# Stage order in blocks, later first weight loads and later group transposes in a one-core attention and expert kernel

## The chip, the cores and the metric

The kernel runs on one core of one Trainium2 chip. Its time is the device time of one execution in microseconds (us); the figure for the kernel before is the median of three runs. The engines are TensorE (PE for its matmuls, PEld for its weight loads), VectorE (DVE), ScalarE (ACT), GpSimd (POOL) and SyncE (SP), which issues the DMAs here. Each engine works through its own queue in order.

## The reference, cut to what matters

```python
scores = scale * np.matmul(q, k.transpose(0, 1, 3, 2))      # 4 x 8 heads, 576 x 64
scores = np.where(block_i >= block_j, scores, -1e9)          # 64-row blocks
attn = softmax(scores); attn_out = np.matmul(attn, v)
x = attn_out.transpose(0, 2, 1, 3).reshape(2304, 512)

P = np.exp(logits - logits.max())                            # logits = x @ w_gate, 8 experts
for _ in range(8):
    P /= P.sum(1, keepdims=True) + 1e-09
    P /= P.sum(0, keepdims=True) + 1e-09
    P *= N / E
for e in range(E):                                           # w1 512 x 1024, w2 1024 x 512
    out += P[:, e:e + 1] * (np.maximum(x @ w1[e], 0.0) @ w2[e])

h = np.maximum(out @ w_in, 0.0)                              # w_in 512 x 2048
return (h * h) @ w_out
```

The second layer's weights arrive as 64-bit numbers; `conv64` turns them into 32-bit ones on the chip while the first layer runs.

## The kernel before, in words

After attention the 2304 tokens are worked on in three groups of 768 tokens (six tiles of 128). A **stage** takes one slice of 256 hidden units for one group. The first layer has 32 stages for each group (8 experts, four slices each), the second has eight, so that there are 120 stages, numbered S = 0 to 119: 0 to 95 are the first layer, 96 to 119 the second.

The first half of a stage are seven **products** (`product(S, j)`, lines 305 to 307, tile `m` in PSUM): a Winograd-like form with seven instead of eight block products, each six matmuls of 384 columns (high and low parts, two halves of k). DVE adds the results up (line 311), ACT and DVE make the high and low part of the hidden units out of the sums: in the first layer ACT line 280 and DVE line 281, in the second DVE line 285 (square of the positive part), ACT line 286 and DVE line 287. The low part's instruction is kept back in a list `wait` and put into DVE's queue by `flush_wait()` at the next product or tile. The second half are six **output tiles** (`output(S, t)`, lines 367 to 369, tile `y`): each six matmuls of 512 columns, followed by one DVE instruction that adds the tile to `acc` (lines 380 and 387). Every output tile of a stage needs the hidden units of all seven products of it.

PE gets the products of stage S woven with the output tiles of stage S - 1, in the order that the string `WEAVE` spells: m is a product, t a tile. Each of these pieces is a beat; at each beat one step of the side work is put into the queues: the next stage's weights (`stage_work`, `conv_a` at lines 165 and 166, `conv_b` at 173 and 174, sums at 149), the forming of the next group's operand (`form`, lines 233 to 240, every 12 beats in the first layer and every 5 in the second), `conv64`, and in stages 5 to 9 `gating` (the eight rounds of normalising P), whose remaining steps are put in at once ahead of tile 0 of stage 8. PSUM holds five product tiles and three output tiles; `y` is shared by the transposes of `x2` and by gating.

At the end of a group's first layer (`s == NMOE - 1`) each finished tile of `acc` is transposed by PE (`x2`, lines 350 to 352, four matmuls, an ACT copy and a DMA), one tile after it was computed.

The attention runs over 16 pairs of heads with six steps r each. The products of stages 0 to 4 are filled in between its steps from about pair 9 on (`fill`, up to `split`). SP's queue first gets the operands of pair 0, then `load("w1", 0)`, `load("w2", 0)` and `load("w1", 1)` (line 137), then q and k of pair 1 (line 522) and v (line 530). A task that makes the first stage's weights (`start`) is stepped from r = `TASK0` on, two steps at a time.

Of the kernel before, what the change touches and what calls it, by code (L numbers as in the profile page):

```python
# [28 lines left out]
NMOE = 32  # L29
# [39 lines left out]

FILL = 1.05  # L70

TASKS = 2

TASK0 = 9
READY = 3

FIRST = (
# [2 lines left out]
)  # L80

WEAVE = "mmtmtmtmtmtmt"

DLO = (0, 3, 6, 9, 12)

# [4 lines left out]
EARLY = 4  # L90
# [5 lines left out]
def fused_kernel(ctx: ExitStack, tc: tile.TileContext, q, k, v, wg, w1, w2, u1, u2, ident, out):  # L96
# [32 lines left out]
    def load(nm, S):  # L129
        if S >= len(stages):  # L130
            return
        s = stages[S][1]
        if s >= NMOE:
            drain(slow)
        t = raw[nm, S] = rawp.tile([128, 1024], F32, tag=nm, name="raw" + nm, bufs=2 if nm == "w1" else 1)
        src = (w1 if nm == "w1" else w2)[s] if s < NMOE else wf[nm][s - NMOE]
        nc.sync.dma_start(out=t, in_=src)
# [133 lines left out]
    late = deque()  # L271
# [17 lines left out]
    def flush_wait():  # L289
        while wait:  # L290
            wait.popleft()()
# [52 lines left out]
    def x2(q, t):  # L344

        a = acc[q % 2][:, t]
        p = extra["py"].tile([128, 512], F32, tag="y", name="x2t")
        for kk in range(KD):
            d = slice(kk * 128, (kk + 1) * 128)
            nc.tensor.transpose(p[:, d], a[:, d], idn)  # L350
        nc.scalar.activation(out=a, in_=p, func=ACTF.Copy)
        nc.sync.dma_start(out=xdram[q + NG][:, t], in_=a)

    def output(S, t):
        g, s, q = stages[S]
        flush_wait()
        while S not in ready_b:
            assert step_of(side)
        first = q == 0 and s < 8
        if q == 0 and s == 8:  # L360
            drain(gate)
        pool, tag = (extra["py"], "y") if "py" in extra else (extra["ps"], "g")
        p = pool.tile([128, 512], F32, tag=tag, name="y")
        bh, bl = wb[S]
        for f in range(2):
            hh, hl = (z[:, t * 128:(t + 1) * 128] for z in ht[S][f])
            nc.tensor.matmul(p, hh, bh[:, f], start=(f == 0), stop=False)  # L367
            nc.tensor.matmul(p, hh, bl[:, f], start=False, stop=False)  # L368
            nc.tensor.matmul(p, hl, bh[:, f], start=False, stop=(f == 1))  # L369

        a = acc[1 if first and s >= 4 else q % 2][:, t]
        e = s // 4
        tile_no = g * GT + t
        pe = prob[:, tile_no, e % NEXP:e % NEXP + 1]
        if s == NMOE or (first and s % 4 == 0):
            nc.scalar.activation(out=a, in_=p, func=ACTF.Copy)
        elif s == 0:
            nc.scalar.activation(out=a, in_=p, func=ACTF.Copy, scale=pe)
        elif s > NMOE or first:
            nc.vector.tensor_tensor(out=a, in0=p, in1=a, op=ALU.add)  # L380
        else:
            if q == 0 and s == 8:
                nc.scalar.activation(out=a, in_=a, func=ACTF.Copy, scale=prob[:, tile_no, 0:1])
                nc.vector.scalar_tensor_tensor(
                    out=a, in0=acc[1][:, t], scalar=prob[:, tile_no, 1:2], in1=a, op0=ALU.mult, op1=ALU.add
                )
            nc.vector.scalar_tensor_tensor(out=a, in0=p, scalar=pe, in1=a, op0=ALU.mult, op1=ALU.add)  # L387
        if late:
            x2(*late.popleft())
        if s == NMOE - 1:  # L390
            late.append((q, t))
        if s == NST - 1:
            r0 = tile_no * 128
            nc.sync.dma_start(out=out[r0:r0 + 128, :], in_=a)
# [4 lines left out]
    def piece(fn, us=0.0, need=None):  # L399
        pieces.append((need, us, fn))  # L400

    def products(S):
        res = []
        for j in range(7):
            def fn(j=j):
                product(S, j)
                if j == 0:
                    load("w1", S + 2)
                else:
                    conv_a(S + 1, PRODUCTS[j - 1][1])  # L410
                if j == 6:
                    conv_a(S + 1, PRODUCTS[6][1])
            res.append((0, 1.03, fn))
        return res

    def outputs(S):
        return [(0, 1.37, lambda t=t: output(S, t)) for t in range(GT)]
# [9 lines left out]
    def step_of(queue):  # L427
        while queue:
            if next(queue[0], "end") != "end":
                return True  # L430
            queue.popleft()
        return False

    def drain(queue):
        while step_of(queue):
            pass
# [17 lines left out]
    def begin(S):  # L454
        side.append(stage_work(S))
        g, s, q = stages[S]
        layer = s >= NMOE
        at, every = FORM[layer]
        if s - (NMOE if layer else 0) == at and q + 1 < 2 * NG:
            forming.append(fetch(q + 1))  # L460
            pace[0] = every

    for S in range(len(stages) + 1):
        a = products(S) if S < len(stages) else []
        b = outputs(S - 1) if S else []
        if a:
            piece(lambda S=S: begin(S))
        for z in WEAVE:
            src = a if z == "m" else b
            if src:  # L470
                pieces.append(src.pop(0))
        pieces += a + b
        if S == EARLY:
            split = len(pieces)
# [23 lines left out]
    def attention():  # L498
        with ExitStack() as es:
# [17 lines left out]
            def load_qk(n):  # L517
                for nm, src, w in (("k", k, SEQ), ("q", q, 9 * 128)):
                    t = qkv.tile([128, w], F32, tag=nm, name=nm)
                    raws[nm, n] = t  # L520
                    if n:
                        nc.sync.dma_start(out=t, in_=src[n])
                if n == 0:

                    for nm, c0, c1 in FIRST:
                        nc.sync.dma_start(out=raws[nm, 0][:, c0:c1], in_=(q if nm == "q" else k)[0, :, c0:c1])

            def load_v(n):
                t = raws["v", n] = vp.tile([128, 640], F32, tag="v", name="v")
                nc.sync.dma_start(out=t, in_=v[n])  # L530
# [134 lines left out]
            def logits_part(n):  # L665

                b, kk = divmod(n, 4)
                p = ps.tile([128, 512], F32, tag="g", name="lp")
                u = max(9 * b, 2 * GT)
                todo = []  # L670
                while u < 9 * (b + 1):
                    t, h = divmod(u, 2)
                    m = min(2 - h, 9 * (b + 1) - u)
                    todo.append((t, slice(64 * h, 64 * (h + m)), u - 9 * b, m))
                    u += m
                for t, rows, i, m in todo:
                    nc.tensor.matmul(
                        p[rows, t * NEXP:(t + 1) * NEXP], xs[:, i:i + m].rearrange("p b c -> p (b c)"),
                        wgt[:, kk], start=True, stop=True,
                    )  # L680
                while todo:
                    rows, t0 = todo[0][1], todo[0][0]
                    while todo and todo[0][1] == rows:
                        t1 = todo.pop(0)[0] + 1
                    o = prob[rows, t0:t1]
                    x = p[rows, t0 * NEXP:t1 * NEXP].rearrange("p (t e) -> p t e", e=NEXP)
                    if kk == 0:
                        nc.vector.tensor_copy(out=o, in_=x)
                    else:
                        nc.vector.tensor_tensor(out=o, in0=x, in1=o, op=ALU.add)  # L690
# [11 lines left out]
                nc.gpsimd.memset(pb[:, POFF[b] + width(b):POFF[b] + width(b) + 64], 0.0)  # L702
            nc.sync.dma_start(out=idn, in_=ident)
            nc.sync.dma_start(out=wgt, in_=wg)
            load("w1", 0)
            load("w2", 0)
            load("w1", 1)
            total = PAIRS * R
            budget = [0.0]
            later = []  # L710
# [15 lines left out]
            def do_fill(r):  # L726
                if r >= TASK0:
                    for _ in range(TASKS):
                        step_of(tasks)
                budget[0] = min(budget[0] + FILL, 2.0)  # L730
                if budget[0] > 0 and formed:
                    budget[0] = fill(budget[0], split)
# [23 lines left out]
            def do_loads(r):  # L756
                n, i = divmod(r, R)
                if later:
                    logits_part(later.pop())
                if i == 0 and n + 1 < PAIRS:  # L760
                    load_qk(n + 1)
                if r >= VSTEP and (r - VSTEP) % R == 0 and (r - VSTEP) // R < PAIRS:
                    load_v((r - VSTEP) // R)

# [141 lines left out]
```

## Time and profile before

| | before |
|---|---|
| median of three runs | 2143.82 us (2142.67 to 2145.21) |
| profiled execution: its time, its span | 2144.16 us, 2142.4 us |
| PE busy | 2105.8 us, 98% |
| PE weight loads busy | 1845.3 us, 86% |
| DVE busy | 1590.9 us, 74% |
| POOL busy | 1575.3 us, 74% |
| ACT busy | 916.2 us, 43% |
| mean granted TensorE clock | 0.995 of 2.4 GHz |

The span runs from the first to the last instruction of the profiled execution. PE's busy time is a sum of matmuls that overlap, with ends that are modelled: where PE sits at 100%, its pace is read from the distance between the starts of matmuls, not from how long each is shown. In a timeline a line shows the start, the length, the engine, the line of the program and, in brackets, how long the engine had been idle and what released it.

### The profile page before, as it was taken

The numbers are of one execution on the slowest core, as the hardware profiler recorded it, in microseconds if no ns is written. First come the engines' busy times: TensorE is split into PE (matmuls) and PEld (weight loads), VectorE is DVE, ScalarE is ACT, GpSimd is POOL, SyncE is SP. The second block draws the span as 40 slices with busy tenths as digits, with TensorE's granted clock in tenths as the row PEclk, the third lists the DMA queues.
The fourth block names the chain that finished last, engine by engine and source line by source line (L and its number), as shares of the span: only waits on it lengthen the run. The fifth ranks groups of instructions, "written<-read, shape, count | busy, mean of one in ns | idle before, by whom it ended". The sixth has DMA issues, their size and how long they took to land.

```text
span 2142.4 us, 32197 instructions
## 1 busy us (share of the span) xinstructions
PE 2105.8 (98%) x10835; PEld 1845.3 (86%) x10835; DVE 1590.9 (74%) x2890; ACT 916.2 (43%) x2267; POOL 1575.3 (74%) x1767
## 2 busy tenths in 40 slices
PE   8999999999999999999999999999999999999998
PEld 6777888888888988888889889898888888888887
DVE  6666678777778667778777767777887667878776
ACT  7766443334343443333434344343343443343432
POOL 3264465878888777778888767778787768878874
PEclk9999999999999999999999999999999999999999
DMA  4433122232232322332323233233222232131211
GB/s 159 136 103 116 53 69 69 89 108 90 84 99 74 120 92 84 99 104 84 99 84 99 79 109 99 84 108 95 87 85 70 70 104 74 64 123 60 99 60 50
DMA packets 80710, 194.58 MB, mean 91 GB/s; under 512 B 26144, under 2 KB 27296, under 8 KB 80544
## 3 DMA queue, kind: packets, MB, share of 16 engines
q1 hardware_dynamic: 80544, 192.53, 28.2%
q8 instruction: 85, 1.39, 0.3%
q14 instruction: 81, 0.66, 0.1%
HBM read 169.95 MB, written 20.97 MB: 89 GB/s over the span
## 4 chain that ended last, share of the span: by engine, by line
PE 88%; DVE 8%; ACT 2%; issue 1%; POOL 0%; DMA 0%; SPq 0%; DVEq 0%; POOLq 0%; ACTq 0%
PE y L369 14%; PE y L368 14%; PE y L367 14%; PE m L306 12%; PE m L307 12%; PE m L305 12%; PE sc L540 3%; PE pv L650 2%; PE T L610 2%; DVE c L285 2%; DVE h L287 2%; DVE c L311 1%; ACT h L286 1%; DVE acc L380 1%; DVE mu L311 0%
## 5 line engine op out<-in xcount | busy, mean ns | idle before, releaser
L367 PE MATMUL y<-b,h 128*128 128x512 f32 x1440 | 566.8, 394 | 19.2 <-ACT h L286 18.0
L369 PE MATMUL y<-b,h 128*128 128x512 f32 x1440 | 574.7, 399 | 0.3 <-DVE h L281 0.3
L305 PE MATMUL m<-x,ah 128*128 128x384 f32 x1680 | 569.9, 339 | 0.0
L368 PE MATMUL y<-b,h 128*128 128x512 f32 x1440 | 569.0, 395 | 0.0
L306 PE MATMUL m<-x,ah 128*128 128x384 f32 x1680 | 566.4, 337 | 0.0
L307 PE MATMUL m<-x,al 128*128 128x384 f32 x1680 | 562.8, 335 | 0.0
L166 POOL TENSOR_TENSOR al<-sum,ah 128x256 fp32r<-128x256 f32 x480 | 391.4, 830 | 223.7 <-ACT ah L165 203.2
L280 ACT ACTIVATE h<-c 128x384 fp32r<-128x384 f32 x384 | 201.8, 526 | 739.5 <-DVE c L311 739.4
L387 DVE SCALAR_TENSOR_TENSOR acc<-y,prob,acc 128x512 f32<-128x512 f32 x516 | 383.9, 744 | 80.0 <-PE y L369 79.0
L166 POOL TENSOR_TENSOR al<-raww,ah 128x256 fp32r<-128x256 f32 x360 | 296.6, 824 | 189.9 <-ACT ah L165 144.6
L281 DVE SCALAR_TENSOR_TENSOR h<-c,h 128x384 fp32r<-128x384 f32 x384 | 275.4, 717 | 187.1 <-ACT h L280 186.7
L306 PEld LDWEIGHTS m<-x,ah 128*128 128x128 f32 x1680 | 316.3, 188 | 34.9 <-issue 1.8
L305 PEld LDWEIGHTS m<-x,ah 128*128 128x128 f32 x1680 | 316.4, 188 | 31.4 <-issue 1.1
L174 POOL TENSOR_TENSOR b<-raww,b 128x512 fp32r<-128x512 f32 x240 | 324.4, 1352 | 20.7 <-ACT b L173 20.1
L369 PEld LDWEIGHTS y<-b,h 128*128 128x128 f32 x1440 | 270.1, 188 | 65.1 <-DVE h L287 5.9
L367 PEld LDWEIGHTS y<-b,h 128*128 128x128 f32 x1440 | 270.9, 188 | 61.1 <-ACT h L286 24.2
L307 PEld LDWEIGHTS m<-x,al 128*128 128x128 f32 x1680 | 316.0, 188 | 0.0
L368 PEld LDWEIGHTS y<-b,h 128*128 128x128 f32 x1440 | 270.3, 188 | 35.2 <-issue 0.9
L165 ACT ACTIVATE ah<-sum 128x256 fp32r<-128x256 f32 x480 | 183.5, 406 | 147.1 <-POOL sum L149 142.6
L149 POOL TENSOR_TENSOR sum<-raww 128x256 f32<-128x256 f32 x240 | 213.4, 889 | 0.0
L311 DVE TENSOR_TENSOR c<-m,u 128x384 f32<-128x384 f32 x240 | 131.9, 550 | 38.7 <-PE m L307 38.4
L173 ACT ACTIVATE b<-raww 128x512 fp32r<-128x512 f32 x240 | 148.7, 620 | 0.0
(90 smaller groups left out, 2264.5 us busy)
## 6 DMA issues: line engine op xcount, KB each, us to landing
raww<-w_t SPq DMA_DIRECT2D x192, 512.0 KB, 3.6
raww<-w1f SPq DMA_DIRECT2D x24, 512.0 KB, 3.3
raww<-w2f SPq DMA_DIRECT2D x24, 512.0 KB, 3.3
q<-q_d SPq DMA_DIRECT2D x15, 576.0 KB, 4.5
raw<-w_in_bits SPq DMA_DIRECT2D x16, 512.0 KB, 5.1
raw<-w_out_bits SPq DMA_DIRECT2D x16, 512.0 KB, 4.6
acc<-xd SPq DMA_DIRECT2D x30, 256.0 KB, 4.2
v<-v_p SPq DMA_DIRECT2D x16, 320.0 KB, 4.9
```

Of the source, the lines that this page charges most:

```text
L149: nc.gpsimd.tensor_tensor(out=t[:, o], in0=x, in1=y, op=op)
L166: nc.gpsimd.tensor_tensor(out=lo, in0=src, in1=hi.bitcast(F32), op=ALU.subtract)
L174: nc.gpsimd.tensor_tensor(out=lo[:, f], in0=src, in1=hi[:, f].bitcast(F32), op=ALU.subtract)
L280: nc.scalar.activation(out=hh, in_=x3, func=ACTF.Relu)
L281: wait.append(lambda: nc.vector.scalar_tensor_tensor(out=hl, in0=x3, scalar=0.0, in1=hh.bitcast(F32), op0=ALU.max, op1=ALU.subtract,))
L305: nc.tensor.matmul(p, ah[:, k2], bh[:, k2], start=(k2 == 0), stop=False)
L306: nc.tensor.matmul(p, ah[:, k2], bl[:, k2], start=False, stop=False)
L307: nc.tensor.matmul(p, al[:, k2], bh[:, k2], start=False, stop=(k2 == 1))
L367: nc.tensor.matmul(p, hh, bh[:, f], start=(f == 0), stop=False)
L368: nc.tensor.matmul(p, hh, bl[:, f], start=False, stop=False)
L369: nc.tensor.matmul(p, hl, bh[:, f], start=False, stop=(f == 1))
L387: nc.vector.scalar_tensor_tensor(out=a, in0=p, scalar=pe, in1=a, op0=ALU.mult, op1=ALU.add)
```

## The change

Three things are changed. From stage 5 on a stage's pieces are put into PE's queue as four products, three tiles, three products and three tiles (`BLOCKS`) instead of woven one by one; stages 0 to 4 keep `WEAVE`. The loads of the first two stages' weights are taken out of the head of SP's queue and put at step 3 of pairs 1, 2 and 3, and the task that uses them starts at r = 15 instead of 9. The transposes of a group's tiles come two tiles later than before while the group's last stage runs.

```diff
+WFIRST = {1: ("w1", 0), 2: ("w2", 0), 3: ("w1", 1)}
-TASK0 = 9
+TASK0 = 15
 WEAVE = "mmtmtmtmtmtmt"
+BLOCKS = "mmmmtttmmmttt"
...
-        if late:
-            x2(*late.popleft())
         if s == NMOE - 1:
             late.append((q, t))
+        if len(late) > (2 if s == NMOE - 1 else 0):
+            x2(*late.popleft())
...
-        for z in WEAVE:
+        for z in WEAVE if S <= EARLY else BLOCKS:
             src = a if z == "m" else b
             if src:
                 pieces.append(src.pop(0))
...
             nc.sync.dma_start(out=wgt, in_=wg)
-            load("w1", 0)
-            load("w2", 0)
-            load("w1", 1)
...
                 if i == 0 and n + 1 < PAIRS:
                     load_qk(n + 1)
+
+                if i == 3 and n in WFIRST:
+                    load(*WFIRST[n])
```

## Rows read from the trace of the kernel before

**Rows 1.** Page, part 1: engine, busy us, share of the span, instructions.

```profile
PE 2105.8 (98%) x10835; PEld 1845.3 (86%) x10835; DVE 1590.9 (74%) x2890; ACT 916.2 (43%) x2267; POOL 1575.3 (74%) x1767
```

**Rows 2.** Timeline of PE, one first-layer stage: start, length, instruction.

```profile
1000.81 0.33 PE L305 MATMUL m<-x,ah 128*128 128x384 f32 x1
...
1002.89 0.39 PE L367 MATMUL y<-b,h 128*128 128x512 f32 x1
...
1004.28 0.33 PE L305 MATMUL m<-x,ah 128*128 128x384 f32 x1
...
1016.45 0.33 PE L305 MATMUL m<-x,ah 128*128 128x384 f32 x1
```

**Rows 3.** Waits of PE, whole span: us in total, times, longest us.

```profile
PE y L367 <- ACT h L286: 18.0, 17, 2.0
```

**Rows 4.** Timeline of PE: second layer's first product; one stall of its stages.

```profile
1724.47 0.33 PE L305 MATMUL m<-x,ah 128*128 128x384 f32 x1
...
1811.47 0.50 PE L367 MATMUL y<-b,h 128*128 128x512 f32 x1 [1.98 <-ACT h L286]
```

**Rows 5.** Timeline of PE, the closing tiles: second tile, sixth, last matmul.

```profile
2131.64 0.39 PE L367 MATMUL y<-b,h 128*128 128x512 f32 x1
...
2137.09 0.39 PE L367 MATMUL y<-b,h 128*128 128x512 f32 x1
...
2138.22 0.39 PE L369 MATMUL y<-b,h 128*128 128x512 f32 x1
```

**Rows 6.** Timeline of PE, a group's end: one transpose and the next tile.

```profile
722.51 0.60 PE L350 MATMUL x2t<-idn,acc 128*128 128x128 f32 x4
...
724.00 0.39 PE L367 MATMUL y<-b,h 128*128 128x512 f32 x1
```

**Rows 7.** Groups of DVE, stage 109 (1945.1 to 1962.7): busy us, mean ns, idle before.

```profile
L285 DVE SCALAR_TENSOR_TENSOR c<-c 128x384 f32<-128x384 f32 x5 | 5.4, 1074 | 0.2
L380 DVE TENSOR_TENSOR acc<-y,acc 128x512 f32<-128x512 f32 x6 | 4.1, 679 | 0.0
L287 DVE TENSOR_TENSOR h<-c,h 128x384 fp32r<-128x384 f32 x4 | 3.2, 803 | 1.9 <-ACT h L286 1.8
L311 DVE TENSOR_TENSOR c<-m,u 128x384 f32<-128x384 f32 x2 | 1.1, 550 | 0.2 <-PE m L307 0.2
```

**Rows 8.** Waits of DVE, whole span.

```profile
DVE h L287 <- ACT h L286: 55.0, 93, 0.6
```

**Rows 9.** Timeline of DVE, last stage, line 285 while POOL is idle.

```profile
2122.77 0.56 DVE L285 SCALAR_TENSOR_TENSOR c<-c 128x384 f32<-128x384 f32 x1
```

**Rows 10.** Stage 109: us, busy of PE, PEld, DVE, ACT, POOL; clock, DMA share, GB/s.

```profile
1945.10:1962.70 17.60, 16.06 (x80) 13.95 (x79) 15.08 (x23) 6.91 (x17) 15.65 (x17) 1.00 0.18 61
```

**Rows 11.** Timeline, last stage: first matmuls of a tile and of the product behind.

```profile
2121.98 0.39 PE L367 MATMUL y<-b,h 128*128 128x512 f32 x1
...
2123.37 0.33 PE L305 MATMUL m<-x,ah 128*128 128x384 f32 x1
```

**Rows 12.** Stretch in the last stage, columns as in rows 10.

```profile
2120.00:2128.00 8.00, 8.00 (x41) 7.07 (x39) 5.64 (x11) 1.05 (x2) 0.00 (x0) 1.00 0.01 2
```

**Rows 13.** Timeline of PE: first scores of attention pairs 1, 2 and 3.

```profile
14.82 1.43 PE L540 MATMUL sc<-k,q 128*128 128x128 f32 x4 [2.39 <-DMA q<-q_d]
...
27.59 1.03 PE L540 MATMUL sc<-k,q 128*128 128x128 f32 x4
...
38.88 1.03 PE L540 MATMUL sc<-k,q 128*128 128x128 f32 x4
```

**Rows 14.** Timeline of SP's queue: the three first weight loads.

```profile
5.44 1.38 SPq L137 DMA_DIRECT2D raww<-w_t  x3
```

**Rows 15.** Stretches behind two stalls, columns as in rows 10.

```profile
15.40:18.80 3.40, 3.40 (x12) 2.66 (x11) 1.51 (x7) 1.57 (x5) 0.00 (x0) 0.51 0.63 242
...
356.70:360.20 3.50, 3.50 (x12) 3.11 (x11) 2.23 (x4) 2.66 (x6) 2.74 (x4) 0.51 0.01 2
```

**Rows 16.** Timeline, gating's last product of sums ahead of tile 0 of stage 8.

```profile
355.61 0.39 PE L827 MATMUL gc<-cs,ones 128*128 128x8 f32 x2 [3.15 <-DVE cs L823]
```

## The prediction

> **What bounds the kernel now.** I read the page first: PE is busy for 98% of the span [rows 1], so only two things can pay: gaps in PE, and PE's own pace. The pace is read from a timeline of PE in a quiet first-layer stage [rows 2]: the first product of one stage starts at 1000.81, that of the next at 16.45, so a stage lasts 15.64 us. Two products in a row take 2.08 (1000.81 to 1002.89), a tile 1.39 (1002.89 to 1004.28); 7 x 1.04 + 6 x 1.39 = 15.62 is the stage. Nothing is waited for, and the first layer repeats this length nearly everywhere; there an order of pieces can gain only if it changes the pace itself.
>
> Then the waits of PE: 18.0 us in 17 waits of the first matmul of a tile for the high part of the second layer's hidden units [rows 3], up to 2 us each [rows 4]. How much of the second layer that is: from its first product at 1724.47 [rows 4] to the last matmul at 2138.22 [rows 5] are 413.75 us. 24 stages of 15.64 are 375.4, the six closing tiles without their last matmul 6 x 1.39 - 0.23 = 8.1, six group transposes 6 x 0.45 = 2.7 (one transpose and a product take 1.49 [rows 6], less 1.04). What is left, 27.6 us, are these stalls with the slow matmuls behind them. So the second layer is paced by the chain product, DVE sum, square, ACT copy, low part, tile, and the first layer by PE alone.
>
> **Order in blocks: the second layer's stalls.** Before, between the end of a stage's last product and its first tile lie one old tile and two products, 1.39 + 2.08 = 3.5 us. In blocks there lie three tiles and four products, 3 x 1.39 + 4 x 1.04 = 8.3 us. I walk DVE's queue from the start of the block of three products, with the durations of a crowded stage [rows 7]: sums 0.55, square 1.07, low part 0.80, tile 0.68. Product 1 is there at 1.2 (1.04 and the hand-over, an estimate); sum, square, two sums, low part, square, sum, low part, square end at 8.2; ACT's copy keeps DVE waiting 0.59 [rows 8], the last low part ends at 9.6, the first tile's add at 10.3. The next stage's tiles start at 3.1 + 4.2 + 4.2 = 11.4. The hidden units (9.6) and the first of the three y buffers (10.3) are in time, by 1.1 us. In the same order only one of the four 0.59 waits is left in a stage; the others now have sums of the next product behind them.
>
> Two things stay late. At the very end six tiles follow directly on three: the closing tile 0 starts at 7.2 on that scale and needs tile 3's buffer, free at 8 with 0.56 for squares and low parts [rows 9] and POOL idle, at 10 otherwise: 1 to 2 us, 1.5 taken. And where the next group's operand is formed (14 parts, one every 5 beats of 13, so 5.4 stages in each of two groups), DVE has 7 x 0.55 + 4 x 1.07 + 4 x 0.80 + 6 x 0.68 + 0.55 + 0.59 = 16.5 us of work in a stage of 15.5: its lag grows 1.0 a stage, 5.4 in a group, of which 1.1 is slack: 9 us lost in the two groups at this end. With 0.56 for all eight it has 13.6 and loses nothing. The measured stage held 15.08 of DVE work [rows 10]; with one wait that is 15.7, near the pace, so I take 2.5. Gain: 27.6 - 1.5 - 2.5 = 23.6, between 16.6 and 26.6.
>
> **Order in blocks: PE's pace.** A tile between two products takes 1.39, also in the last stage [rows 11], where POOL does nothing and ACT 1.05 of 8 us [rows 12]. Six closing tiles follow one another, and there the second to sixth start 2131.64 to 2137.09 apart, 5.45 / 4 = 1.36 each [rows 5]. DVE's adds are present in both, so it is the change between products and tiles that costs, not a neighbour engine. In blocks four of six tiles follow a tile: 4 x 0.0275 = 0.11 a stage. For products the rows' rounding leaves 0 to 0.04; I take 0.015. 115 stages (5 to 119) x 0.125 = 14.4, less the 11 forming stages that DVE may pace (1.4): 13.0, between 0 and 14.4.
>
> The Trainium skill (TensorE: Matmul & The Clock Gate, section "Wait — 56ns, not 53.3ns?") says that back-to-back matmuls start N / 2.4 GHz + about 2.5 ns apart, N alone deciding. By that rule no order changes the pace, this term is 0 and the sum 13 smaller. The trace does not follow it here: 1.39 and 1.36 for the same six matmuls of 512 columns [rows 5, 11].
>
> **First loads.** Pair 1's first scores waited 2.39 us for q [rows 13]. Ahead of it in SP's queue stood three weight loads, 1.38 us of issue [rows 14] and 1.5 MB of transfer. Without them q is issued 1.4 earlier and shares the DMA engines with 1.5 MB less; the stall goes. Behind this idle time TensorE's clock was granted at 0.51, its lower level of 1.2 GHz, for 3.4 us [rows 15], and pair 1 took 12.77 against 11.29 of pair 2 [rows 13]: 1.5 more. Gain 2.39 to 3.9 if the clock holds, less up to 0.2 for the task's ACT and POOL steps, which move from pairs 1 and 2 to pairs 2 and 3, where they find the same gaps beside the softmax. I take 3.3 (2.2 to 3.9). The moved loads have free buffers, so nothing in SP's queue (q, k and v of a pair ahead, the attention's stores) stands behind a wait; w1 is read six steps, some 11 us, after its issue. Products only start after pair 8, so the later task delays none. If the loads did crowd pair 2's q, a stall like the 2.39 would be back.
>
> **Gating.** Tile 0 of stage 8 now comes after four products of stage 9 instead of two, so two more of gating's 60 steps are already in the queues when the rest is put in. PE waited 3.15 there for the reciprocal, product and sums on DVE [rows 16]; now only the fourth product's sum and the column sums are left, some 2 us. The clock fell to 0.51 behind it too [rows 15]; 3.5 us at half pace cost 1.7. Against it: the other rounds' sums meet runs of products, where DVE is busiest; up to 1. Gain 1.5 (-1 to 3).
>
> **Transposes two tiles later.** Four small matmuls a tile as before; no queue gets more. The transpose now needs a y buffer while tiles come in threes: after tile 4 it takes tile 3's, which DVE frees up to 0.4 late. The copy and store come two tiles later, but the group is read back only a layer of stages later. Cost 0.5 for three groups, 0 to 2.
>
> **Sum.** 23.6 + 13.0 + 3.3 + 1.5 - 0.5 = 40.9. From the profiled execution's 2144.16 that is 2103.3; the median lies 0.3 below it: **2103**.
>
> **The rivals.**
> The pace doesn't follow the order: 1.36 belongs to the quiet end. For it: in the closing tiles POOL and ACT are silent throughout. Against: they nearly were in a stretch with the slow tiles [rows 11, 12]. The 13.0 fall away: 2116.
>
> DVE becomes the bound of the forming stages. For it: squares take 1.07 with POOL on and 0.56 with POOL off [rows 7, 9], POOL holds 15.65 of 17.60 us [rows 10], and a faster PE squeezes both into less. If the low parts stretch like the squares, DVE needs 7 x 0.55 + 8 x 1.07 + 4.1 + 0.55 + 0.59 = 17.6, the old length: 5.4 x 2.1 less the slack of 1.1 are 10.2 us a group, 20.4 in two, of which 2.5 + 1.4 are counted above: 2120. The Trainium skill (SBUF — State Buffer, section "Who interferes with whom") names the reason: a VectorE instruction with two SBUF inputs and a GpSimd one that reads SBUF take the shared port exclusively, one fully waiting. The stretch from 0.56 to 1.07 agrees. Both rivals together: 2132.
>
> Slower: tiles in threes outrun DVE. Place: the first tile of each block of three, which needs the buffer of the first tile of the block before. In the first layer DVE frees it about 5 us early by the walk above, so it decides only once DVE's lag in every stage passes 5 us, as with the 64-bit conversion and the group operand on top. With stages of 15.5 + 0.5 = 16.0 the 91 first-layer stages cost 91 x 0.36 = 33 us more; the second layer, before at 15.64 + 27.6 / 24 = 16.8, would give back 19 and the start 3: 2155.
>
> Nothing: the stalls return at the blocks' ends and the pace stays: 2142.
>
> **How the numbers follow.** Forecast 0.65 (its own range 2095 to 2111), pace 0.13 (2116), DVE 0.12 (2120), both 0.02 (2132), slower 0.05, nothing 0.03. Faster by over 0.2% (4.3 us, about what a measurement of this kernel can tell from no change): 0.92, same 0.03, slower 0.05. The range takes in the forecast with its bounds and the first two rivals: 2094 to 2121.
>
> **What would show it.** Stage length: 15.52 in the first layer (15.64 if the pace rival holds); tiles 1.39, 1.36, 1.36 in a block. Waits of PE for line 286: under 3 us in all, or late in the forming stages. Second layer to the last matmul: 388 to 390 us. No wait of PE for q at pair 1, pair 1 near 11.3, no low clock there; gating's wait near 2. Wrong, if PE waits for DVE at a block's first tile, or if first-layer stages are longer than 15.64.

## The result, and the profile after

The changed kernel takes 2110.98 us (median of four runs, 2110.31 to 2112.36) against 2143.24 us before: 0.985 of the time, 95% interval 0.984 to 0.986, so 32 us less. The forecast was 2103, with a range of 2094 to 2121; without the rivals' times its range was 2095 to 2111, and the result lies at the upper end of that. The profiled execution has a span of 2109.7 us, 32.7 less than before, and all that follows divides these 32.7 up.

The page's first part, as in [rows 1]: PE is at 99%, and DVE is busy for 59 us longer with the same 2890 instructions.

```profile
PE 2086.4 (99%) x10835; PEld 1846.3 (88%) x10835; DVE 1650.1 (78%) x2890; ACT 921.2 (44%) x2267; POOL 1565.5 (74%) x1767
```

Two groups of DVE account for these 59 us (39 and 27 more; all others together lose 7): the low parts of the first layer and the squares of the second. The lines show the count, the busy time and the mean in ns of one, first of the kernel before, then of the changed one.

```profile
L281 DVE SCALAR_TENSOR_TENSOR h<-c,h 128x384 fp32r<-128x384 f32 x384 | 275.4, 717 | 187.1 <-ACT h L280 186.7
L285 DVE SCALAR_TENSOR_TENSOR c<-c 128x384 f32<-128x384 f32 x96 | 72.6, 756 | 3.3
```

```profile
L284 DVE SCALAR_TENSOR_TENSOR h<-c,h 128x384 fp32r<-128x384 f32 x384 | 314.8, 831 | 6.9 <-ACT h L283 5.1
L288 DVE SCALAR_TENSOR_TENSOR c<-c 128x384 f32<-128x384 f32 x96 | 99.5, 1036 | 1.7
```

Both kinds read two operands from SBUF. The adds of a tile, which read one of theirs from PSUM, kept their means of 744 and 682 ns. The squares will matter below.

First I looked for the waits of PE over the whole span (us in total, times, longest). The 18.0 us behind ACT's line 286 of [rows 3] are gone, the wait for q of [rows 13] too. In their place stands DVE's line 383, the add that frees a tile's buffer: 3.7 of its 5.6 us fall in the second layer, 1.9 in stages 5 to 8, where gating runs.

```profile
PE y L370 <- DVE acc L383: 5.6, 8, 1.6
...
PE x2t L353 <- ACT acc L354: 2.2, 1, 2.2
PE gc L830 <- DVE cs L826: 2.1, 1, 2.1
PE y L370 <- DVE acc L390: 1.0, 2, 0.5
```

Then PE's pace, in the timeline of a quiet first-layer stage, as in [rows 2]. The rows are the first matmul of product 1, of product 2, of tiles 1, 2 and 3, of the product behind them, and of the next stage:

```profile
993.48 0.33 PE L308 MATMUL m<-x,ah 128*128 128x384 f32 x1
994.55 0.33 PE L308 MATMUL m<-x,ah 128*128 128x384 f32 x1
...
997.67 0.39 PE L370 MATMUL y<-b,h 128*128 128x512 f32 x1
...
999.06 0.39 PE L370 MATMUL y<-b,h 128*128 128x512 f32 x1
...
1000.43 0.39 PE L370 MATMUL y<-b,h 128*128 128x512 f32 x1
...
1001.79 0.33 PE L308 MATMUL m<-x,ah 128*128 128x384 f32 x1
...
1009.05 0.33 PE L308 MATMUL m<-x,ah 128*128 128x384 f32 x1
```

A stage lasts 993.48 to 1009.05, 15.57 us; it was 15.64. Its three tiles take 1.39, 1.37 and 1.36, within a hundredth of the forecast. But the first product takes 1.07, and so does each first product behind tiles (1.066, by the distances between starts in the trace; before it was 1.044). The other engines are busier than in the stretch of [rows 12] (the stage's length, then busy time of PE, PEld, DVE, ACT and POOL, the granted clock, DMA share and GB/s):

```profile
993.48:1009.05 15.57, 15.57 (x79) 14.09 (x78) 13.62 (x21) 6.32 (x15) 14.21 (x16) 1.00 0.20 64
```

The second layer, from its first product to the last matmul, as in [rows 4, 5], now takes 392.1 us instead of 413.75; 388 to 390 were forecast. Its two largest waits for a tile's buffer stand between the ends, in the first stages of the second and third group (104 and 112), each at the first tile of a block:

```profile
1713.39 0.33 PE L308 MATMUL m<-x,ah 128*128 128x384 f32 x1
...
1848.68 0.47 PE L370 MATMUL y<-b,h 128*128 128x512 f32 x1 [1.22 <-DVE acc L383]
...
1976.03 0.47 PE L370 MATMUL y<-b,h 128*128 128x512 f32 x1 [1.61 <-DVE acc L383]
...
2105.52 0.39 PE L372 MATMUL y<-b,h 128*128 128x512 f32 x1
```

The start: the first scores of pairs 1, 2 and 3, as in [rows 13], and a stretch of pair 1 (busy time of PE, PEld, DVE, ACT, POOL, then the granted clock, DMA share and GB/s). Pair 1 starts at 12.26 instead of 14.82, takes 11.07 instead of 12.77, and the clock stays at its full level.

```profile
12.26 1.03 PE L543 MATMUL sc<-k,q 128*128 128x128 f32 x4
...
23.33 1.03 PE L543 MATMUL sc<-k,q 128*128 128x128 f32 x4
...
34.35 1.03 PE L543 MATMUL sc<-k,q 128*128 128x128 f32 x4
```

```profile
12.20:15.60 3.40, 3.40 (x23) 2.48 (x20) 3.37 (x17) 3.28 (x10) 2.10 (x3) 1.00 0.75 246
```

By the starts of the stages' first products the 32.7 us divide up so (gains are positive):

| term | forecast | measured |
|---|---|---|
| second layer's stalls | 23.6 | 22.3 |
| PE's pace in 115 stages, 0.067 each | 13.0 | 7.7 |
| start, up to stage 5 | 3.3 | 5.2 |
| gating, stages 5 to 10, both included | 1.5 | -0.5 |
| transposes, three groups | -0.5 | -4.0 |
| single stalls of six other first-layer stages | not counted | 2.0 |
| sum | 40.9 | 32.7 |

### The profile page after: what moved, and what is told of

The parts are those of the page before. It is cut to its first block, busy times and chain, and to the rows that moved or that the text cites. A ratio compares the mean times of both kernels' runs of the same rounds, so it can differ in the third digit from the quotient of the medians.

```text
span 2109.7 us, 32655 instructions
## 1 busy us (share of the span) xinstructions
PE 2086.4 (99%) x10835; PEld 1846.3 (88%) x10835; DVE 1650.1 (78%) x2890; ACT 921.2 (44%) x2267; POOL 1565.5 (74%) x1767
## 4 chain that ended last, share of the span: by engine, by line
PE 91%; DVE 7%; ACT 1%; issue 1%; POOL 0%; DMA 0%; SPq 0%; ACTq 0%; DVEq 0%; POOLq 0%
PE y L371 15%; PE y L372 15%; PE y L370 15%; PE m L310 13%; PE m L308 13%; PE m L309 13%; PE sc L543 3%; PE pv L653 2%; PE T L613 2%; DVE c L288 2%; DVE acc L383 1%; DVE h L290 1%; DVE c L314 1%; ACT h L289 1%; DVE h L284 1%
## 5 line engine op out<-in xcount | busy, mean ns | idle before, releaser
L169 POOL TENSOR_TENSOR al<-sum,ah 128x256 fp32r<-128x256 f32 x480 | 402.3, 849 | 152.5 <-ACT ah L168 139.4
L390 DVE SCALAR_TENSOR_TENSOR acc<-y,prob,acc 128x512 f32<-128x512 f32 x516 | 374.9, 744 | 114.6 <-PE y L372 112.5
L177 POOL TENSOR_TENSOR b<-raww,b 128x512 fp32r<-128x512 f32 x240 | 318.6, 1328 | 181.7 <-ACT b L176 181.6
L169 POOL TENSOR_TENSOR al<-raww,ah 128x256 fp32r<-128x256 f32 x360 | 285.1, 792 | 78.7 <-ACT ah L168 69.4
L284 DVE SCALAR_TENSOR_TENSOR h<-c,h 128x384 fp32r<-128x384 f32 x384 | 314.8, 831 | 6.9 <-ACT h L283 5.1
L152 POOL TENSOR_TENSOR sum<-raww 128x256 f32<-128x256 f32 x240 | 194.1, 809 | 0.0
L319 ACT ACTIVATE m<-m 128x384 f32<-128x384 f32 x120 | 58.8, 490 | 229.0 <-PE m L310 228.7
```

What stands on the lines that cost most here:

```text
L152: nc.gpsimd.tensor_tensor(out=t[:, o], in0=x, in1=y, op=op)
L169: nc.gpsimd.tensor_tensor(out=lo, in0=src, in1=hi.bitcast(F32), op=ALU.subtract)
L177: nc.gpsimd.tensor_tensor(out=lo[:, f], in0=src, in1=hi[:, f].bitcast(F32), op=ALU.subtract)
L284: wait.append(lambda: nc.vector.scalar_tensor_tensor(out=hl, in0=x3, scalar=0.0, in1=hh.bitcast(F32), op0=ALU.max, op1=ALU.subtract,))
```

## Experiments

All kernels compute the whole reference. Each edit is made to the changed kernel; times are set against its 2111.0, or as ratios to the kernel before, which took 2143.8 to 2144.2 when it was run again beside them.

### The order alone undone

```diff
-        for z in WEAVE if S <= EARLY else BLOCKS:
+        for z in WEAVE:
```

> Only the order of the pieces is undone: all stages are woven one by one again, the late loads and the late transposes stay. Theory (the blocks bring the second layer's stalls and some 0.07 us of pace in every stage, the start brings 5.2 us by itself): stage 15.64 us, second layer back to 413 to 414 us from its first product to the last matmul, product 0 of stage 0 near 133.9; time 2143.2 - 5.2 = 2138 us, give or take 1.5. Rival (the gain of the second layer comes from the shifted phase against the side work, not from the order): second layer near 395, time near 2120.

Measured: 2138.7 us, ratio 0.9975 (0.9963 to 0.9986). The stage is back at 15.64 us, the second layer at 411.6, and the waits are those of before (waits of PE, us, times, longest):

```profile
PE y L370 <- ACT h L289: 17.6, 17, 1.9
```

So the order brings some 28 of the 32 us. The second layer is 2.1 us shorter than before, 1.4 below what was expected; 1.6 of that is stage 103 alone, in which the clock fell to 0.50 for 3.4 us in the kernel before and not here. The rival, a second layer near 395, is out: the shift of the start leaves at most 2.1 of the 21.6 us. The transposes two tiles later cost the woven order nothing: 2.7 us a group, as before.

### The start undone, and half undone

```diff
+            load("w1", 0)
+            load("w2", 0)
+            load("w1", 1)
             total = PAIRS * R
...
-                if i == 3 and n in WFIRST:
-                    load(*WFIRST[n])
```

In the first of the two kernels TASK0 is 9 again, in the second it stays at 15.

> Only the start is undone: the three weight loads stand ahead of pair 1 again and the task starts at r = 9. Theory (the start's gain is the 2.4 us wait for q, the low clock behind it and nothing of the later stages): the wait of 2.4 us for q and a stretch at 1.2 GHz behind it are back, pair 1 takes 12.8; time 2111.0 + 5.2 = 2116 us (2114.5 to 2117). Rival (the shift is made up again before the products start): 2111 to 2112.

> The three loads stand ahead of pair 1 again, but the task stays at r = 15. Theory (pair 1 was slow by the clock behind the wait, not by the task): the wait of 2.4 us is back, the clock falls behind it and pair 1 takes 12.5 to 12.8 without the task beside it, pair 2 11.0 and pair 3 11.3; time as with both undone, 2116 us. Rival (the task's POOL and ACT steps made pair 1 slow): pair 1 takes 11.1 to 11.3 and the time is 2113 to 2114.

Measured: 2117.3 us (ratio 0.9879, 0.9864 to 0.9894) and 2115.9 us (0.9869, 0.9854 to 0.9884), 6.3 and 4.9 above. The wait for q is back in both. The rows are pair 1's first scores and the stretch behind it, first of the kernel with TASK0 at 9, then of the one at 15:

```profile
14.82 2.04 PE L543 MATMUL sc<-k,q 128*128 128x128 f32 x4 [2.64 <-DMA q<-q_d]
```

```profile
14.80:18.20 3.40, 3.38 (x11) 2.69 (x12) 1.30 (x6) 0.45 (x1) 0.00 (x0) 0.50 0.79 312
```

```profile
15.28 1.11 PE L543 MATMUL sc<-k,q 128*128 128x128 f32 x4 [2.37 <-DMA q<-q_d]
```

```profile
14.80:18.20 3.40, 2.92 (x19) 2.54 (x20) 1.78 (x9) 0.97 (x4) 0.00 (x0) 1.00 0.89 283
```

The first is as expected in these rows, with a time 0.3 above its range: 0.50 of the clock, its 1.2 GHz level, behind an idle 2.64 us, and pair 1 takes 12.75. The second is not: behind an idle 2.37 us the clock stays at its full level, and pair 1 takes 11.09. So a wait of this length makes the lower level possible, not certain. The theory expected 12.5 to 12.8 here, and what came is the pair 1 of the rival; that the time agrees with the theory's 2116 is luck. That pair 1 was slow by the clock and not by the task rests on sizes: 3.4 us at half pace are 1.7, the whole difference of 12.75 and 11.09, while the task's steps show as 0.28 in one later pair, pair 2 with TASK0 = 9 and pair 3 with 15. A run with the task early and the clock full would have shown it directly; there was none.

The totals hold two more parts that the edits didn't aim at. Up to stage 5 the two kernels are 7.4 and 5.7 us behind, of which pair 1 with its wait is 4.2 and 3.0; the other 3.1 and 2.6 lie in pairs 9 to 11, where the clock's lower level lasted 13.6 us instead of 6.8 (0.50 from 113.8 to 124.0 in the first, from 111.4 to 118.1 in the changed kernel). And gating's wait of 2.06 to 2.07 us is there in both, as in the changed kernel, but the clock stayed full behind it, and stages 9 and 10 took 1.3 us less. So 6.3 and 4.9 are not the price of the start alone: what the rows show of it is the wait and, where the clock fell, 1.7 more.

### Transposes one tile later, and in pairs in the next stage

```diff
-        if len(late) > (2 if s == NMOE - 1 else 0):
+        if len(late) > (1 if s == NMOE - 1 else 0):
             x2(*late.popleft())
```

> Only the transposes are put back to one tile later, in blocks. Theory (what they cost now, 3.5 us in each of the first two groups and 5.1 in the third instead of 2.7, comes from the three shared y buffers and from ACT's copies queued behind the second layer's squares, not from how late they come): costs within 1 us a group of these, time 2109 to 2114. Rival (one tile later PE waits at each transpose for DVE's add of the tile just made): 4 to 6 us a group more, 2120 or above.

Measured: 2114.1 us (ratio 0.9864, 0.9847 to 0.9880). The two stages of a group's end take 35.1, 35.1 and 36.5 us, against 34.7, 34.7 and 36.2 with the change: 1.1 us more in all. The profiled execution is 1.7 us longer, and the other 0.7 lie ahead of stage 5; the rest of the 3 us between the medians is in no profile. The rival's price is out. But the wait is of the kind that the rival named (waits of PE), DVE's add in place of ACT's copy, so the theory's reason is not shown by this run:

```profile
PE x2t L353 <- DVE acc L390: 4.5, 3, 2.4
```

In the changed kernel the wait is for ACT. Timeline of the third group's end, where stage 96 is already a second-layer stage: ACT's copy that frees a buffer (line 354) stands in its queue behind the copy of a hidden unit (line 289), and that waits for DVE's square (line 288).

```profile
1729.15 0.52 ACT L289 ACTIVATE h<-c 128x384 fp32r<-128x384 f32 x1 [1.33 <-DVE c L288]
...
1730.19 0.57 ACT L354 ACTIVATE acc<-x2t 128x512 f32<-128x512 f32 x1
1730.82 0.66 PE L353 MATMUL x2t<-idn,acc 128*128 128x128 f32 x4 [2.18 <-ACT acc L354]
```

If the second block of tiles is the bad place, the transposes should be cheap in the first block of the next stage:

```diff
-        if len(late) > (2 if s == NMOE - 1 else 0):
-            x2(*late.popleft())
+        if s != NMOE - 1 and t < 3:
+            for _ in range(2):
+                if late:
+                    x2(*late.popleft())
```

> All six transposes of a group are made in the next stage, two behind each of the first three tiles, where DVE and ACT have caught up. Theory (the transposes' extra cost comes from the second block of tiles, where the three buffers wait for DVE's adds and for ACT's copies queued behind the second layer's squares): a group costs 2.7 to 3 us instead of 3.5, 3.5 and 5.1; time 2107 to 2108. Rival (two transposes and a tile in a row are too much for three buffers wherever they stand): 3.5 us a group and more, 2111 or above.

Measured: 2108.8 us (ratio 0.9839, 0.9825 to 0.9854). A group's transposes cost 3.0, 3.0 and 3.4 us, and PE no longer waits for the transposes' copies at all. The rival is out, and the place is what cost. The third group and the time are 0.4 and 0.8 us above the theory's figures.

### Three changes a stage, and one

```diff
-BLOCKS = "mmmmtttmmmttt"
+BLOCKS = "mmmttmmttmmtt"
```

> The blocks are three, two and two products, each followed by two tiles: three changes from products to tiles and back in a stage, between the six of the woven order (15.64 us) and the two of the new one (15.57). A stage without any change would be 7 x 1.038 + 6 x 1.362 = 15.44. Theory (a change has a price that grows with the runs around it: a first tile 0.027 more, a second 0.010, products behind one tile 0.006, behind three 0.029): first-layer stages of 15.57 to 15.64, tiles of 1.39 and 1.37. Rival (the price of a change is fixed, 0.033 as in the woven order): 15.54.

Measured: 2117.5 us (one run), quiet stages of 15.64 us. Timeline of first matmuls: tile, tile, product, product, tile.

```profile
1000.97 0.39 PE L370 MATMUL y<-b,h 128*128 128x512 f32 x1
...
1002.36 0.39 PE L370 MATMUL y<-b,h 128*128 128x512 f32 x1
...
1003.73 0.33 PE L308 MATMUL m<-x,ah 128*128 128x384 f32 x1
...
1004.80 0.33 PE L308 MATMUL m<-x,ah 128*128 128x384 f32 x1
...
1005.84 0.39 PE L370 MATMUL y<-b,h 128*128 128x512 f32 x1
```

The tiles take 1.39 and 1.37, the product behind two tiles 1.07, the second 1.04. Three changes thus cost as much as six in the woven order: over the 1.360 and 1.040 that tiles and products settle at, there a first tile pays 0.029 and a product behind a single tile 0.004, 0.033 in all; behind two tiles the product pays 0.026 and the second tile 0.012 more, 0.067 in all. The rival's fixed price (15.54) is out.

The run also tells something of the second layer's stalls. In this order two tiles and three products, some 5.9 us, lie between a last product and its first tile, against 3.5 in the woven order and 8.3 in the new one. The wait for the hidden units is in between too, 18.0 us before [rows 3], none with the change, and here:

```profile
PE y L370 <- ACT h L289: 2.9, 4, 1.4
```

```diff
-BLOCKS = "mmmmtttmmmttt"
+BLOCKS = "mmmmmmmtttttt"
```

> All seven products and then all six tiles: one change a stage. Theory (the price of a change stops growing behind three tiles): quiet first-layer stages of 15.50 us, tiles 1.39, 1.37 and four of 1.36, first product 1.067. Rival (the price grows on with the run, so that a stage keeps it): 15.57. In the second layer six tiles on three buffers make PE wait for DVE's adds, 1.5 to 3 us a stage; total 2130 to 2170.

Measured: 2340.8 us (one run), far above what was expected: PE waits for the tile buffers in nearly every second-layer stage and most first-layer ones (waits of PE). In the first layer DVE has the sums of seven products ahead of the first tile's add, and the fourth tile has no buffer. The waits are not all of the 230 us: the clock was at its lower level for 118 us of the time after 300 us (0.92 in the mean of the second layer), against 7 in the changed kernel, and 111 us more at half pace cost some 55.

```profile
PE y L370 <- DVE acc L390: 77.9, 87, 2.6
PE y L370 <- DVE acc L383: 65.6, 24, 4.4
```

The 15.50 us of a stage can therefore not be read off. The products can: the first behind six tiles takes 1.066, no more than behind two or three, as the theory says. So the price of a change has two levels, 0.033 with one tile and 0.067 with two or more.

### What is left at a group's turn

```diff
-FORM = {False: (12, 12), True: (2, 5)}
+FORM = {False: (12, 12), True: (2, 4)}     # or (1, 5)
```

> In the second layer a part of the next group's operand is formed every 4 beats instead of 5, so that none is left over to be put in at once at the group's turn; more of it falls on each forming stage. Theory (the waits left at the group's turn, 4.6 us in stages 103 to 105 and 111 to 113, are DVE's lag piled up while forming): the lag piles up faster, the waits move into the stages before the turn and stay at 3 to 7 us, time 2110 to 2113. Rival (they come from the parts put in at once at the turn): they vanish, 2107.

> The second layer's forming starts one stage sooner at the same density, so that none is left over at the group's turn and DVE has a stage without forming ahead of it. Theory (lag piled up): the lag comes to light one stage sooner or is worked off in part, 2 to 4 us of waits stay, time 2108.5 to 2110.5. Rival (parts put in at once): the waits vanish, stages 104 and 112 fall to 15.6, time 2106.5.

Measured: 2115.5 us (ratio 0.9868, 0.9851 to 0.9884) and 2112.5 us (0.9855, 0.9841 to 0.9870). With nothing left over for the turn, the waits do not vanish. At every 4 beats they move to stages 101 to 104 and 109 to 112 (15.8 to 17.3 us each) and the second layer takes 395.9 us; with the forming one stage sooner they too come sooner (102 to 104, 107 to 112) and it takes 393.5. The parts put in at the turn are not the cause. The lag theory stands, though both times are 2 to 3 us above what it expected. The stretch of stages 100 to 103 in the changed kernel shows how full DVE and POOL are, with the group of DVE's squares in it (mean ns of one), as in [rows 7]:

```profile
1780.80:1843.10 62.30, 62.30 (x313) 56.26 (x312) 58.64 (x85) 26.34 (x64) 61.57 (x63) 1.00 0.18 60
```

```profile
L288 DVE SCALAR_TENSOR_TENSOR c<-c 128x384 f32<-128x384 f32 x16 | 18.6, 1162 | 0.3
```

POOL is busy for 61.57 of 62.3 us and DVE for 58.64, and a square takes 1.16 us, against 1.07 in the crowded stage before and 0.56 beside an idle POOL [rows 7, 9]. That the long squares make the lag is argued from these sizes; no run changed the squares alone.

```diff
-                rest.pop()(nc.vector if z - 1 in DLO else nc.gpsimd)
+                rest.pop()(nc.vector if z - 1 in DLO and q <= NG else nc.gpsimd)
```

> In the second layer the low parts of the next group's operand are all made by POOL; before, five of fourteen went to DVE. Theory (the 4.6 us of waits left around the group's turn are DVE's lag, and these five instructions of some 0.8 us in each of two groups are about as long as the lag): waits in the second layer fall under 1.5 us, time 2106.5 to 2108. Rival (DVE is slowed by POOL on the shared port, so that more work on POOL gives the lag back): 2110 to 2114.

Measured: 2116.4 us (ratio 0.9876, 0.9861 to 0.9891), the rival's side and beyond. The second layer takes 398.0 us, 5.9 more than with the change. Some 1.7 of these are a fall of the clock in stage 112 (0.50 from 1980.2 to 1983.5), behind two waits in a row. Waits of PE in it:

```profile
PE m L310 <- POOL al L169: 2.5, 3, 1.2
PE y L370 <- DVE acc L383: 2.2, 4, 0.8
```

The wait for DVE's add is smaller (3.7 with the change), but now POOL is late with the weights' low parts. In these stages the two engines are near their limit together, and work moved from DVE to POOL came back as a wait of PE. The Trainium skill (SBUF — State Buffer, section "Who interferes with whom") says that a VectorE instruction with two SBUF inputs and a GpSimd instruction that reads SBUF exclude each other on a shared port. The lengths agree with it; no run here measures the port alone.

### Gating under the woven order

```diff
-        for z in WEAVE if S <= EARLY else BLOCKS:
+        for z in WEAVE if S <= 8 else BLOCKS:
```

> Stages 5 to 8, in which the eight rounds of normalising run beside the products, are woven again; blocks begin at stage 9. Theory (in blocks the rounds' sums meet runs of tiles or products and cost 2.4 us in stages 6 to 8, while the shorter wait at stage 9 comes from the four products ahead of it): stages 5 to 8 take 65.2 us instead of 67.5, stage 9 stays at 19.7, time 2108.7. Rival (what stages 6 to 8 lose is gained in stage 9, one for one): no gain, 2111.

Measured: 2108.0 us (ratio 0.9835, 0.9819 to 0.9852). Timeline, the first products of stages 5, 9 and 10:

```profile
280.81 0.33 PE L308 MATMUL m<-x,ah 128*128 128x384 f32 x1
```

```profile
346.01 0.33 PE L308 MATMUL m<-x,ah 128*128 128x384 f32 x1
```

```profile
364.27 0.33 PE L308 MATMUL m<-x,ah 128*128 128x384 f32 x1
```

Stages 5 to 8 take 65.2 us instead of 67.5, as expected. What cost the 2.3 us in blocks are tiles without a buffer: three waits of PE for DVE's add, 1.9 us in all, of which the woven kernel has none. Gating's small product holds one of the three buffers, and its sums stand in DVE's queue; which of the two weighs more was not tested. PE's timeline of the changed kernel shows one of these waits, and the one that is left of [rows 16] with the stretch behind it:

```profile
311.94 0.50 PE L370 MATMUL y<-b,h 128*128 128x512 f32 x1 [0.85 <-DVE acc L383]
...
353.75 0.59 PE L830 MATMUL gc<-cs,ones 128*128 128x8 f32 x2 [2.06 <-DVE cs L826]
```

```profile
353.70:357.10 3.40, 3.35 (x9) 2.77 (x10) 1.85 (x4) 1.34 (x3) 3.40 (x5) 0.50 0.00 0
```

Stage 9 took 18.3 us here instead of 19.7, since the clock stayed at its full level behind a wait of 2.2 us. That part is not the edit's doing: in the two kernels with the start undone the clock stayed full there too, without this edit.

### The three edits together

Stages 5 to 8 woven, transposes in pairs, forming on POOL.

> The three edits together: stages 5 to 8 woven, the transposes in pairs in the next stage, the second layer's low parts on POOL. Theory (the three act in different stretches, so that they add up): 2111 - 2.3 - 3.5 - 4 = 2101 us, 2100 to 2103. Rival (forming on POOL gains nothing): 2105.

Measured: 2113.5 us (ratio 0.9862, 0.9847 to 0.9876). The parts add up as they were measured one by one: stages 5 to 8 take 65.2 us and the transposes of the first two groups 3.0, but the second layer takes 395.7 us through the forming on POOL. The theory's 2101 counted 4 us of gain for that edit, which alone had cost 5.4; and the profiled execution is 2.7 us behind the changed kernel's up to stage 5, ahead of all three edits. Weaving to stage 8 and pairing the transposes without that edit was not run; each alone came out 2 to 3 us under the changed kernel, with intervals that overlap its own.

## Why the forecast was right, and where it was off

The sum missed by 8.2 us: the pace by 5.3, the transposes by 3.5, gating by 2.0 and the stalls by 1.3, against 2.0 not counted and 1.9 at the start on the other side. That these two fell on the good side was not foreseen.

**Second layer's stalls: right.** 22.3 of 27.6 us gone, 23.6 forecast. The mechanism is the one walked through: 8.3 us instead of 3.5 between a last product and its first tile. The order alone brings it, and with 5.9 us between them most of the wait had gone. 1.6 of the 22.3 are a fall of the clock behind a stall, which the sum had among the slow matmuls. What stays is 5.3 us instead of 4.0. I had the place, DVE's lag while the next operand is formed, and the buffer on which it shows; I took 2.5 between 0 and 9 and 4.8 stayed, most of it one stage later than I put it, once the lag has used up the slack of several stages. The end kept 0.5 instead of 1.5. One sign that I had named for being wrong, PE waiting for DVE at a block's first tile, did come, in stages 104 and 112 and, at 0.25 us and less, next to them: the walk through DVE's queue holds in the other stages, not where the lag has piled up.

**PE's pace: the mechanism right, the size off.** This is the term that missed most, 7.7 of 13.0. The step that failed is "For products the rows' rounding leaves 0 to 0.04; I take 0.015". In the woven order a product never stands behind more than one tile, so no row could show that it pays 0.026 behind two or more, against 0.004 behind one. A stage's products got 0.03 dearer, not 0.015 cheaper, and its tiles saved 0.09 instead of 0.11, since the second of a block takes 1.37: 15.52 forecast, 15.57 measured. Six changes and three cost the same, as the order with three showed; the gain comes from having two. The Trainium skill's spacing (TensorE: Matmul & The Clock Gate, section "Wait — 56ns, not 53.3ns?"), by which the columns of a matmul alone decide, is not what these runs show either: the same tile takes 1.39, 1.37 and 1.36 within one block.

**Start: right, and low.** 5.2 against 3.3, beyond my upper bound of 3.9. The wait for q (2.4) and the low clock behind it (1.7) both went; I had counted the second by half, and from too small a difference: pair 2, against which I took it, holds the 0.28 of the task. The remaining 0.9 lies in pairs 9 to 11, where the clock's lower level came and went between kernels with the same work there, for 6.8 to 13.6 us in all; it lasted 10.2 us before and 6.8 in the changed kernel. That part is luck, and without it the term is 4.3.

**Gating: the sign wrong.** The wait at stage 9 fell from 3.15 to 2.06 as forecast, but the clock fell behind it as before, and stages 6 to 8 lost 2.4. I had put the danger at up to 1 and in DVE's queue; what showed were waits for a buffer that DVE frees, and gating takes one of the three. Stage 10 gained 1.0, since a wait of 0.6 for ACT's line 280 went; without it the term would be -1.5.

**Transposes: too cheap.** 4.0 lost instead of 0.5, beyond my bound of 2. 2.3 of the 4.0 are the third group's. I checked the tile's buffer and DVE's add, and overlooked that the transposes' own buffers are freed by ACT, whose queue stands there behind the second layer's squares. The first two groups lost 0.8 each, 0.5 of it a tile that waits for DVE's add (line 390), which I had put at up to 0.4. Pairs in the next stage cost 1.2 over the old price in all instead of 4.0.

**Not counted:** six first-layer stages lost 0.1 to 0.6 us each before, at a tile or just behind one. In blocks they run at 15.57, which gave 2.0.

**The rivals.** The pace rival is out: in blocks tiles speed up beside busy engines. DVE as the bound of the forming stages came true by a quarter of its price (4.8 of 20.4). The mechanism of the slower rival, tiles in threes that outrun their buffers, is how these 4.8 show, in stages 104 and 112 and next to them; with six tiles in a row it ruled the kernel.

## What to carry to other kernels

Where PE waits at a fixed place for a chain through two other engines, more of PE's own work between producer and consumer takes the wait away, as long as the buffers of the run in between last; three buffers carried three tiles here and not six. An order of pieces has a price at each change, and it must be read in the order that is planned: a row of the old order shows only the changes that the old order has. A transpose or a small product put into a ring of buffers has to be followed to the engine that frees it, with all that stands ahead of it in that engine's queue.

## What the runs showed of the hardware

- Six matmuls of 512 columns take 1.39 us behind matmuls of 384, 1.37 as the second such group and 1.36 from the third on; six of 384 take 1.04 us, 1.044 behind one group of 512 and 1.066 behind two, three or six. What makes it was not found: no wait goes with it, and a tile between products took 1.39 beside an idle POOL too [rows 11, 12].
- PE's clock at its 1.2 GHz level for 3.4 us followed idle times of 2.06 and 2.64 us in some kernels and not those of 2.37 and 2.2 in others; ahead of the same product of gating an idle time of 2.06 was followed by it in one kernel and not in another.
- A DVE square of 128 x 384 from SBUF took 0.56 us beside an idle POOL and 1.16 in the mean beside one that was busy for 99% of the stretch. Over the whole kernel the two DVE groups that grew by most (717 to 831 ns, 756 to 1036) read both operands from SBUF; the adds with one in PSUM kept their 744 and 682.
